# The first block's probabilities: transposed by a float32 matmul instead of by DMA, and new DMA durations in the ordering clock

## The chip, the cores and the metric

The kernel runs on one core of a Trainium2 chip. The metric is the device time of one execution in microseconds (us), lower is better. A core has five engines that work side by side, each in the order of its own queue: PE (matmuls; PEld is its weight load), DVE (vector work), ACT (activations and scaled copies), POOL (a second, slower vector engine) and SP, which here only issues DMA transfers.

## The reference

Causal attention, then a gated two-layer network on its output, all float32. Sizes: 4 batches, 12 heads, 448 positions, 64 per head; 1792 tokens of 768, hidden width 2048.

```python
scores = scale * np.matmul(q, k.transpose(0, 1, 3, 2))
scores = np.where(mask, -1000000000.0, scores)
scores = scores - np.max(scores, axis=-1, keepdims=True)
attn = np.exp(scores)
attn = attn / (np.sum(attn, axis=-1, keepdims=True) + 1e-09)
attn_out = np.matmul(attn, v)
x = attn_out.transpose(0, 2, 1, 3).reshape(B * S, H * D)
h = x @ w_in
g = h * (1.0 / (1.0 + np.exp(-1.702 * h)))
out = g @ w_out
```

## The kernel before

**Tiling.** The sequence of each batch is cut into two blocks, of 4 and of 3 chunks of 64 rows (`blocks`, eight in all, n = 0 to 7). A block has six units, one for each pair of heads (`unit`, L1134). The two heads of a pair lie in the two halves of the 128 partitions. After the attention of a block come its `h_slice`s (L1254: x times w_in, eight slices of 256 hidden columns, with the gate) and its `out_tile`s (L1307: g times w_out, tiles of 128 tokens in two halves of 384 columns). Products in the network and most in the attention are made of float16 pairs (a high part and a rest, "hi" and "lo", three matmuls for one).

**One unit.** For each run of two chunks: scores on PE into `ps_s` (L1060 in float32 for batch 0, L1068 in float16 pairs for the others), mask and row minimum on DVE into the float32 tile `z` (L1091), exponential and row sum on ACT (L1105), the sum scaled on POOL or DVE (L1163), its reciprocal on DVE (L1169). `p_pair` (L1117) then writes the probabilities, z times the reciprocal, as two float16 tiles in `p16`: hi on ACT or DVE (`scaled`, L476 or L478), lo on DVE (`rest`, L481). When all runs of the unit are there, one DMA transpose on SP's queue (L1179) turns `p16` into `PT`, and PE multiplies by the values (L1197, the "PV" matmuls) into `ps_v`. After every second unit ACT and DVE write `xT` (L1215 to L1224; for block 1 it is `xT1`). `p16` and `PT` have two buffers each, `z` has one place for each chunk, `ps_h` has three banks, which the `h_slice`s use.

**The weights.** They come in 64-bit words; `to_f32` (L555) makes float32 of them (L565 to L608, on ACT and DVE), `gram` (L621) estimates their size on PE, `split` writes float16 pairs. This runs beside the attention of the first two blocks, and loads on SP's queue feed it.

**What sets the order.** Nothing is ordered by hand. `Ops.add` takes each step with an estimated cost on the engines that could do it, its reads and writes, a priority from `TUNE` and, for transfers, a DMA duration. `Ops.order` (L107) searches 300 rounds over a list planner, with a DMA clock (`DMA_START`, `DMA_END`, `ROWS`, L73) and a PE clock, and emits each step on the engine that the best round gave it. So an altered cost can move steps everywhere, and from one engine to another.

Of the kernel before, what the change touches and what calls it, by code (L numbers as in the profile page):

```python
# [59 lines left out]
class Ops:  # L60
# [9 lines left out]
    HOP = 0.14  # L70
    SECOND = 1e5
    LOAD = 0.68
    DMA_START, DMA_END, DMA_DEPTH = 1.0, 0.8, 8  # L73
    ROWS = 0.19

    def __init__(self):
        self.ops = []
# [239 lines left out]
def pool(n, rate=1.885):  # L317
    return {"POOL": (rate * n + 220) / 1e3}
# [3 lines left out]
def kernel(  # L322
# [451 lines left out]
    def v_batch(b, prio):  # L774
        st = bst[b]
        for j in range(NJ):
            r = min(P, S - j * P)
            add(
                {"SP": Ops.LOAD},
                lambda e, j=j, r=r: nc.sync.dma_start(  # L780
                    out=vraw[:r, j], in_=v[b, :, j * P : j * P + r, :].rearrange("h p d -> p h d")
                ),
                [], [("vraw", j, 0)] + ([("vraw", j, 1)] if r == P else []), prio, dma=2.18 * r / P,
            )
        sqv, sqv_key = col("sqv", 2, 2 * NJ)
# [14 lines left out]
        if not (b == 0 and TUNE["gram_v"]):  # L800
            add(
                dve(2 * NJ),
                lambda e: nc.vector.tensor_reduce(out=sq, in_=sqv, axis=AX.X, op=ALU.max),
                [(sqv_key, j) for j in range(2 * NJ)], [sq_key], prio,
            )
        amx, amx_key = all_max(sq, sq_key, "v", "S" if b else "O", prio)
        st["s_v"], st["s_v_key"] = col("s_v", 2)
        st["i_v"], st["i_v_key"] = col("i_v", 2)
        norm_scale("v", amx, amx_key, st["s_v"], st["s_v_key"], st["i_v"], st["i_v_key"], prio)
# [67 lines left out]
    def k_unit32(u, c0, c1, prio):  # L877

        m = u % 2
        f = q16[:, m * 16 * D : m * 16 * D + 8 * D].bitcast(F32).rearrange("p (j t d) -> p j t d", j=2, d=D)  # L880
        w = 64 * (c1 - c0)
        r = w // 2
        keys = [("q16", m, j) for j in range(4)]
        load_heads(f, k[0, 2 * u : 2 * u + 2, 64 * c0 : 64 * c1], r, [keys[:2], keys[2:]], prio, 0.045 * (c1 - c0))
        got, got_key = turn(f, r, keys, prio)
        kt = kT[u // 2][:, u % 2 * NC : u % 2 * NC + NC].rearrange("p c w -> p (c w)").bitcast(F32)
        add(
            {**act(w, psum=True, rate=1.2), **dve(w, rate=1.2)},
            lambda e: scaled(e, kt[:, 64 * c0 : 64 * c1].rearrange("p (x t) -> p x t", t=2), got, 1.0),
            [got_key], [("kT", u, c) for c in range(c0, c1)], prio,  # L890
        )
        bst[0]["kT", u] = kt

    def q_unit32(n, u, prio):
# [3 lines left out]
        r = 32 * ni  # L898
        f = qf[:, i].rearrange("p (j t) d -> p j t d", j=2)
        keys = [("qf", i, j) for j in range(2)]  # L900
        load_heads(f, q[b, 2 * u : 2 * u + 2, 64 * c0 : 64 * c1], r, [[x] for x in keys], prio, 0.045 * ni)
        got, got_key = turn(f, r, keys, prio)
        t = qT_r.next()
        qt = qT[t].rearrange("p c w -> p (c w)").bitcast(F32).rearrange("p (c j w) -> p c j w", j=2, w=64)
# [63 lines left out]
    def q_pair(n, u, prio):  # L968
# [7 lines left out]
        for a in range(2):  # L976
            for j in range(2):
                keys += [("qf", a, j)]
                add(
                    {"SP": Ops.LOAD},  # L980
                    lambda e, a=a, j=j: nc.sync.dma_start(  # L981
                        out=f[64 * j : 64 * j + 64, a * ni : (a + 1) * ni],
                        in_=q[b, 2 * (u + a) + j, 64 * c0 : 64 * c1].rearrange("(c p) d -> p c d", p=64),
                    ),
                    [], keys[-1:], prio, dma=0.09 * ni,
                )
        sq, sq_key = col("sqq", 2)
        square_sum(
# [128 lines left out]
    def p_pair(i, pi, at, r, r_key, prio):  # L1117
# [13 lines left out]
            zs + [r_key] + keys[0], keys[1], prio,  # L1131
        )

    def unit(n, u, prio):  # L1134
        b, c0, c1 = blocks[n]
        ni = c1 - c0
# [13 lines left out]
        for i0 in range(c0 - c0 % 2, c1, 2):  # L1150
# [5 lines left out]
            for a, i in enumerate(run):  # L1156
# [11 lines left out]
            add(  # L1168
                dve(6 * ln), lambda e, ls=ls, rs=rs: nc.vector.reciprocal(rs, ls), l_keys, [r_key], prio  # L1169
            )  # L1170
            for a, i in enumerate(run):
                at = [where[i, J] for J in range(i // 2 + 1)]
                assert at == list(range(at[0], at[-1] + 1, at[1] - at[0] if at[1:] else 1))
                p_pair(i, pp_i, at, rs[:, a : a + 1], r_key, prio)
        ne = len(places)
        all_keys = [("PT", pi)]
        add(
            Ops.turned(2 * ne),
            lambda e: nc.sync.dma_start_transpose(  # L1179
                out=PT[pi][:, :ne].rearrange("p a g t -> p (a g) t"),  # L1180
# [281 lines left out]
```

## Time and profile before

| what | value |
|---|---|
| median of 3 runs | 640.23 us |
| the runs | 640.47, 640.23, 637.7 us |
| profiled execution, first to last instruction (its span) | 633.9 us |
| busy: PE / DVE / ACT / POOL | 582.6 / 422.4 / 357.2 / 96.6 us |
| mean granted clock of PE | 0.976 of full speed |

The profiled execution has no time of its own beside its span; the runs lie 3.8 to 6.6 us above that span, for what is outside the first and last instruction. Busy shares are means over a program whose stages differ: the strips of the page (busy tenths in 40 slices of about 16 us) show DVE high in the first third and PE high from then on. A granted clock below 1.00 is a mix of PE's two levels, 1.2 and 2.4 GHz.

### The profile page before, as it was taken

Reading aid. Unit: us, or ns where it says so; the run is one execution under the profiler, and the core shown is the slowest. Engines: PE = TensorE matmul, PEld = TensorE weight load, DVE = VectorE, ACT = ScalarE, POOL = GpSimd, SP = SyncE. Lnnn points to the kernel's source line nnn. Section 1 sums busy time; section 2 is a strip of 40 time slices with the busy share of each in tenths; the row PEclk is TensorE's granted clock in tenths of the full one; section 3 lists DMA queues with packets and bytes.
Section 4 is the critical chain, followed back from the end, with each engine's and each line's share of the span. In section 5 each row is a group of like instructions: output and inputs, shape, how many; then the busy total and the mean of one; then the engine's idle time right before and its main releaser. Section 6 shows DMA issues by size and latency. Waiting matters only on the chain. (4 is left out here: it accounts for less than half of the span.)

```text
span 633.9 us, 14759 instructions
## 1 busy us (share of the span) xinstructions
PE 582.6 (92%) x5723; PEld 439.5 (69%) x5723; DVE 422.4 (67%) x1128; ACT 357.2 (56%) x835; POOL 96.6 (15%) x235
## 2 busy tenths in 40 slices
PE   4777688978999999998999999999999999999997
PEld 3555466754588767876678667885679688777964
DVE  4999899999978898977498976769644213101300
ACT  4878888778657776758465565557343223012210
POOL 2233220043202124121021521001000000000000
PEclk9976689999999999999999999999999999999999
DMA  8999969678599687999847798627620040000000
GB/s 276 271 277 293 220 224 284 194 188 166 110 176 190 120 164 124 180 159 173 176 103 135 136 181 160 127 62 130 122 67 2 13 96 1 3 26 26 1 26 26
DMA packets 226407, 85.71 MB, mean 135 GB/s; under 512 B 207137, under 2 KB 216097, under 8 KB 226337
## 3 DMA queue, kind: packets, MB, share of 16 engines
q1 hardware_dynamic: 226336, 84.76, 62.7%
q8 instruction: 45, 0.74, 0.5%
q14 instruction: 26, 0.20, 0.1%
HBM read 41.68 MB, written 5.51 MB: 74 GB/s over the span
## 5 line engine op out<-in xcount | busy, mean ns | idle before, releaser
L1268 PE MATMUL ps_h<-xT,wib 128*128 128x192 f16 (+1 forms) x2304 | 239.3, 261 | 3.5 <-DVE gT L481 3.4
L1333 PE MATMUL ps_o<-wob,gT 128*128 128x384 f16 (+1 forms) x1536 | 233.8, 326 | 5.3 <-DVE wob L481 2.3
L1268 PEld LDWEIGHTS <-wib 128*128 128x128 f16 x2304 | 207.0, 98 | 31.8 <-issue 12.1
L1333 PEld LDWEIGHTS <-gT 128*128 128x128 f16 (+1 forms) x1536 | 131.4, 101 | 87.0 <-issue 12.6
L1105 ACT ACTIVATE z<-z,cols 128x320 f32<-128x320 f32 (+5 forms) x168 | 83.8, 500 | 47.1 <-DVE cols L1091 40.1
L1294 DVE SCALAR_TENSOR_TENSOR ps_h<-t,ps_h 128x512 f32<-128x512 f32 (+1 forms) x64 | 39.9, 624 | 76.5 <-ACT t L1289 76.3
L481 DVE SCALAR_TENSOR_TENSOR p<-z,cols,p 128x384 f16<-128x384 f32 (+3 forms) x168 | 82.6, 523 | 3.0 <-ACT p L476 1.9
L1091 DVE CUSTOM_DVE_ANT_0 z<-ps_s,mask,cols 128x384 f32<-128x384 f32 (+6 forms) x126 | 55.8, 478 | 30.1 <-PE ps_s L1068 30.1
L1289 ACT ACTIVATE t<-ps_h,cols 128x512 f32<-128x512 f32 (+1 forms) x64 | 40.1, 627 | 60.0 <-PE ps_h L1268 59.5
L476 ACT ACTIVATE p<-z,cols 128x128 f16<-128x128 f32 (+3 forms) x108 | 55.3, 538 | 15.4 <-DVE cols L1169 6.7
L1163 POOL TENSOR_SCALAR cols<-cols 128x2 f32<-128x2 f32 (+1 forms) x70 | 20.1, 287 | 208.6 <-ACT z L1105 207.7
L481 DVE SCALAR_TENSOR_TENSOR gT<-ps_h,gT 128x512 f16<-128x512 f32 (+1 forms) x64 | 39.6, 620 | 15.8 <-ACT gT L476 15.7
L476 ACT ACTIVATE gT<-ps_h 128x512 f16<-128x512 f32 (+1 forms) x58 | 31.1, 539 | 28.3 <-DVE ps_h L1294 28.1
L476 ACT ACTIVATE ob<-ps_o,cols 128x384 f32<-128x384 f32 x23 | 13.2, 575 | 59.8 <-PE ps_o L1333 59.8
L1197 PEld LDWEIGHTS <-v 128*64 128x64 f16 x864 | 38.4, 113 | 9.6 <-issue 7.6
L1197 PE MATMUL ps_v<-PT,v 128*64 128x192 f16 (+3 forms) x864 | 41.1, 243 | 4.1 <-DMA PT<-p 4.1
L1068 PE MATMUL ps_s<-kT,qT 128*64 128x192 f16 (+4 forms) x504 | 38.8, 277 | 2.4 <-DVE cols L1091 1.3
L1060 PE MATMUL ps_s<-kT,qT 128*128 128x64 f32 (+6 forms) x84 | 29.3, 468 | 2.6 <-DVE cols L1091 1.9
L1024 POOL TENSOR_SCALAR q<-q 128x512 f16<-128x512 f16 (+1 forms) x30 | 25.2, 841 | 43.0 <-ACT q L476 30.1
L1105 ACT ACTIVATION_READ_ACCUMULATOR z<-z,cols 128x1 f32 x168 | 31.7, 188 | 0.0
L476 ACT ACTIVATE wob<-wob 128x768 f32<-128x768 f32 (+1 forms) x19 | 20.8, 1095 | 15.6 <-DMA wob<-in_moe_w_in_dram 10.6
L1068 PEld LDWEIGHTS <-qT 128*64 128x64 f16 x504 | 19.6, 110 | 13.9 <-issue 9.9
(89 smaller groups left out, 541.1 us busy)
## 6 DMA issues: line engine op xcount, KB each, us to landing
wob<-in_moe_w_in_dram SPq DMA_DIRECT2D x16, 768.0 KB, 6.0
wob<-in_moe_w_out_dram SPq DMA_DIRECT2D x9, 768.0 KB, 5.5
vraw<-in_moe_w_out_dram SPq DMA_DIRECT2D x7, 768.0 KB, 5.4
out_dram<-ob SPq DMA_DIRECT2D x28, 192.0 KB, 2.1
vraw<-in_v_dram SPq DMA_DIRECT2D x12, 384.0 KB, 5.7
kf<-in_k_dram SPq DMA_DIRECT2D x36, 112.0 KB, 2.9
qf<-in_q_dram SPq DMA_DIRECT2D x48, 64.0 KB, 3.2
qf<-in_q_dram SPq DMA_DIRECT2D x48, 48.0 KB, 2.7
```

What stands on the lines that cost most here:

```text
L476: nc.scalar.activation(out=dst, in_=src, func=AF.Copy, scale=sc)
L481: nc.vector.scalar_tensor_tensor(out=dst, in0=src, scalar=sc, in1=hi, op0=ALU.mult, op1=ALU.subtract)
L1024: nc.gpsimd.tensor_scalar(out=dst, in0=src, scalar1=1.0, scalar2=1.0, op0=ALU.mult, op1=ALU.mult)
L1060: nc.tensor.matmul(ps, qt[:, i - c0].rearrange("p j w -> p (j w)"), kt[:, : 64 * (i + 1)], start=True, stop=True)
L1068: nc.tensor.matmul(ps[64 * j : 64 * j + 64], qt[:, g, i - c0, 64 * j : 64 * j + 64], kt[:, : i + 1, 64 * j : 64 * j + 64], start=(g == 0), ...
L1091: lambda e: nc.vector.tensor_tensor_reduce(out=z[:, :w], in0=ps, in1=mask[:, S - w :], scale=c, scalar=3.0e38, op0=ALU.add, op1=ALU.min, a ...
L1105: lambda e: nc.scalar.activation(out=z[:, :w], in_=z[:, :w], func=AF.Exp, bias=m, scale=-1.0, accum_out=l),
L1197: nc.tensor.matmul(ps[64 * j : 64 * j + 64, 64 * (first - c0) : w], vt[:, gv, J, j, :], PT[pi][:, at, gp, 64 * j : 64 * j + 64], start=(t ...
L1268: nc.tensor.matmul(ph[:, t], wib[:, sl, u, gw, t * P : (t + 1) * P], xT[x][:, gx, u, :w], start=(u == 0 and gw + gx == 0), stop=(u == NU - ...
L1289: lambda e: nc.scalar.activation(out=th, in_=ph, func=AF.Tanh, scale=ts[:, sl : sl + 1]),
L1294: lambda e: nc.vector.scalar_tensor_tensor(out=ph, in0=th, scalar=1.0, in1=ph, op0=ALU.add, op1=ALU.mult),
L1333: nc.tensor.matmul(po[o : o + m, :OH], gT[:, f, gg, 64 * r : 64 * r + m], wo_pair(f, gw, nh), start=(f == 0 and gg + gw == 0), stop=(f == ...
```

## The change

For block 0 alone (`TUNE["pet"]`), `p_pair` and the DMA transpose are left out, and `p_turned` is called once for each run of two chunks. POOL or DVE writes `diag`, an identity scaled by the reciprocals, into the same `p16` memory. PE multiplies each 128x128 tile of `z`, as the stationary operand, by `diag` in float32: 2 tiles for the first run of a unit, 4 for the second, into a `ps_h` bank. ACT or DVE copies the hi part from there to `PT`, DVE writes the lo part. That makes 12 runs and 36 such matmuls. `PT` now has four dependency keys instead of one. The second edit replaces the DMA durations that the ordering clock uses: start and end, rows of a transpose, and the loads of q, k and v.

```diff
@@ TUNE @@
+    pet=(0,),
@@ class Ops @@
-    DMA_START, DMA_END, DMA_DEPTH = 1.0, 0.8, 8
-    ROWS = 0.19
+    DMA_START, DMA_END, DMA_DEPTH = 1.23, 0.95, 8
+    ROWS = 0.214
@@ v_batch; k_unit32, q_unit32; q_pair @@
-... dma=2.18 * r / P,
+... dma=2.43 * r / P,
-load_heads(f, ..., 0.045 * ni)
+load_heads(f, ..., 0.062 * ni)
-[], keys[-1:], prio, dma=0.09 * ni,
+[], keys[-1:], prio, dma=0.125 * ni,
@@ new @@
+    def p_turned(run, pi, pp_i, where, rs, r_key, prio):
+        ...
+        add(
+            {**pool(ln * P), **dve(ln * P)},
+            lambda e: by(e).tensor_tensor(
+                out=diag,
+                in0=ident.unsqueeze(1).to_broadcast([P, ln, P]),
+                in1=rs.unsqueeze(2).to_broadcast([P, ln, P]),
+                op=ALU.mult,
+            ),
+            [r_key] + ident_keys, diag_keys, prio,
+        )
+        hb = ps_h_r.next()
+        ps = ps_h[hb][:, : nt * P]
+        def mm(e):
+            for at, J, a, i in tiles:
+                nc.tensor.matmul(
+                    ps[:, (at - p0) * P : (at - p0 + 1) * P], z_of(i)[:, J], diag[:, a], start=True, stop=True
+                )
+        add({"PE": nt * (4 * P / 2.4 + 150) / 1e3}, mm, ...)
+        ...
+        add({**act(nt * P, psum=True), **dve(nt * P)}, lambda e: scaled(e, hi, ps3, 1.0), ...)
+        add(dve(nt * P), lambda e: rest(lo, ps3, 1.0, hi), ...)
@@ unit @@
+            if n in TUNE["pet"]:
+                p_turned(run, pi, pp_i, where, rs, r_key, prio)
+                continue
...
-        all_keys = [("PT", pi)]
-        add(
+        all_keys = [("PT", pi, x) for x in range(4)]
+        if n not in TUNE["pet"]:
+          add(
             Ops.turned(2 * ne),
```

The planner then orders everything anew. In the rows that follow, names carry their buffer numbers, a line number of the changed kernel is higher by 1 up to its L1133 and by 48 or 52 behind `p_turned`, and `ISA` at L1091 (L1092) is the mask and row minimum, whose second row reads out the minimum.

DVE, where the first unit's probabilities are made. Before:

```order
L1169 RECIPROCAL cols_88<-cols_88 128x2
L603 SCALAR_TENSOR_TENSOR wob_61<-wob_61 128x768
L481 SCALAR_TENSOR_TENSOR p160_82<-z_81,cols_88,p160_82 128x128 x2
L1091 ISA z_81,cols_88<-ps_s0_91,mask_87 128x64
L1091 ISA cols_88 128x1
L632 TENSOR_REDUCE cols_88<-ps_o1_98 128x1
L481 SCALAR_TENSOR_TENSOR p160_82<-z_81,cols_88,p160_82 128x2x128
L1091 ISA z_81,cols_88<-ps_s0_91,mask_87 128x128
L1091 ISA cols_88 128x1
L1091 ISA z_81,cols_88<-ps_s1_92,mask_87 128x192
L1091 ISA cols_88 128x1
L481 SCALAR_TENSOR_TENSOR p160_82<-z_81,cols_88,p160_82 128x2x128
```

Now, from the reciprocals of the first unit on:

```order
L1217 RECIPROCAL cols_88<-cols_88 128x2 x2
L482 SCALAR_TENSOR_TENSOR wib_62<-wob_61,cols_88,wib_62 128x6x256
L633 TENSOR_REDUCE cols_88<-ps_o1_98 128x1
L579 TENSOR_SCALAR wob_61<-wob_61 128x768
L444 TENSOR_SCALAR cols_88<-cols_88 128x1
L479 TENSOR_SCALAR kT1_68<-ps_o0_97 128x256
L593 TENSOR_SCALAR wob_61<-wob_61 128x768
L1092 ISA z_81,cols_88<-ps_s0_91,mask_87 128x64
L1092 ISA cols_88 128x1
L1092 ISA z_81,cols_88<-ps_s0_91,mask_87 128x128
L1092 ISA cols_88 128x1
L604 SCALAR_TENSOR_TENSOR wob_61<-wob_61 128x768
```

Between the reciprocals and the second unit's write to `z` there stood two rests of `p16`; now a weight split and other weight work stand there, and the `z` row needs PE's matmuls on the old `z` behind it.

POOL, after its constants. Before:

```order
L542 MEMSET vraw_64 64x768
L1163 TENSOR_SCALAR cols_88<-cols_88 128x2 x2
L457 TENSOR_SCALAR cols_88<-cols_88 128x1
L450 TENSOR_SCALAR cols_88<-cols_88 128x1
L1163 TENSOR_SCALAR cols_88<-cols_88 128x2
L457 TENSOR_SCALAR cols_88<-cols_88 128x1
L450 TENSOR_SCALAR cols_88<-cols_88 128x1
L1163 TENSOR_SCALAR cols_88<-cols_88 128x2 x2
```

Now:

```order
L543 MEMSET vraw_64 64x768
L912 MEMSET qT1_78 64x4x64
L451 TENSOR_SCALAR cols_88<-cols_88 128x1
L1211 TENSOR_SCALAR cols_88<-cols_88 128x2
L1146 TENSOR_TENSOR p160_82<-ident_99,cols_88 128x256 x2
L458 TENSOR_SCALAR cols_88<-cols_88 128x1
L451 TENSOR_SCALAR cols_88<-cols_88 128x1
L1211 TENSOR_SCALAR cols_88<-cols_88 128x2
L1146 TENSOR_TENSOR p161_83<-ident_99,cols_88 128x256
```

The `TENSOR_TENSOR` rows are the scaled identities. They stand between the small scalar steps; 11 of the 12 are on POOL, one is on DVE.

SP, the first transfers. Before:

```order
L652 DMA wob_61<-in_moe_w_in_dram 128x3x512 x2
L856 DMA q16_76<-in_k_dram 128x128 x2
L856 DMA qf_74<-in_q_dram 128x128 x2
L856 DMA q16_76<-in_k_dram 128x128
L856 DMA qf_74<-in_q_dram 128x128
L856 DMA q16_76<-in_k_dram 128x128
L652 DMA wob_61<-in_moe_w_in_dram 128x3x512
L856 DMA qf_74<-in_q_dram 128x128
```

Now:

```order
L857 DMA qf_74<-in_q_dram 128x128 x2
L653 DMA wob_61<-in_moe_w_in_dram 128x3x512 x2
L857 DMA q16_76<-in_k_dram 128x128
L857 DMA qf_74<-in_q_dram 128x128 x2
L857 DMA q16_76<-in_k_dram 128x128 x2
L653 DMA wob_61<-in_moe_w_in_dram 128x3x512
L857 DMA q16_76<-in_k_dram 128x128
L653 DMA wob_61<-in_moe_w_in_dram 128x3x512
```

Two loads of q now stand ahead of the first weight loads, and the second load of the first unit's k (`q16` is its landing place) comes later in the row. Further down, SP's queue has lost six transposes of 12 tiles.

## Rows read from the trace of the kernel before

**Rows 1.** The page: granted clock and DMA share in 40 slices.
```profile
PEclk9976689999999999999999999999999999999999
DMA  8999969678599687999847798627620040000000
```
**Rows 2.** Windows: stretch, length, busy us by engine (count), clock, DMA share, GB/s.
```profile
core 0: us, PE busy (x) PEld busy (x) DVE busy (x) ACT busy (x) POOL busy (x), PEclk, DMA share, GB/s
16.00:32.00 16.00, 12.71 (x104) 9.65 (x104) 15.55 (x52) 13.99 (x38) 4.47 (x9) 1.00 1.14 272
64.00:80.00 16.00, 10.29 (x84) 7.44 (x84) 13.82 (x24) 13.23 (x25) 5.25 (x6) 0.68 0.99 228
16.00:80.00 64.00, 45.87 (x373) 34.63 (x371) 60.45 (x155) 52.78 (x119) 20.23 (x32) 0.79 1.09 266
85.40:182.50 97.10, 86.67 (x786) 62.04 (x785) 91.86 (x210) 75.79 (x151) 20.76 (x44) 0.98 0.82 198
182.50:634.00 451.50, 439.99 (x4477) 335.19 (x4474) 259.23 (x747) 215.76 (x548) 50.55 (x136) 1.00 0.52 98
```
**Rows 3.** Waits of PE, 16 to 182.5 us: total, times, longest.
```profile
PE ps_o L430 <- DVE cols L632: 7.6, 6, 2.8
PE ps_o L621 <- DVE wob L603: 4.9, 5, 1.5
PE ps_v L1197 <- DMA PT<-p: 3.0, 1, 3.0
```
**Rows 4.** Lines by form, 0 to 182.5 us: shapes, count, busy, mean ns, idle before.
```profile
L481 DVE SCALAR_TENSOR_TENSOR p<-z,cols,p 128x128 f16<-128x128 f32 x16 | 5.1, 342 | 0.0
L481 DVE SCALAR_TENSOR_TENSOR p<-z,cols,p 128x256 f16<-128x256 f32 x14 | 6.3, 479 | 0.1
L478 DVE TENSOR_SCALAR p<-z,cols 128x128 f16<-128x128 f32 x4 | 1.0, 281 | 0.0
L478 DVE TENSOR_SCALAR p<-z,cols 128x256 f16<-128x256 f32 x2 | 0.7, 352 | 0.0
L478 DVE TENSOR_SCALAR v<-vraw,cols 128x1024 f16<-128x1024 f32 x4 | 2.9, 753 | 0.1
L478 DVE TENSOR_SCALAR ob<-ps_o,cols 128x384 f32<-128x384 f32 x2 | 1.2, 606 | 0.0
L578 DVE TENSOR_SCALAR wob<-wob 128x768 uint16<-128x768 uint16 x9 | 5.4, 605 | 0.9 <-DMA wob<-in_moe_w_out_dram 0.8
L578 DVE TENSOR_SCALAR wob<-wob 128x1536 uint16<-128x1536 uint16 x4 | 4.1, 1037 | 0.4 <-DMA wob<-in_moe_w_in_dram 0.4
L481 DVE SCALAR_TENSOR_TENSOR wob<-wob,cols 128x768 f16<-128x768 f32 x16 | 16.5, 1034 | 0.7 <-ACT wob L476 0.6
L481 DVE SCALAR_TENSOR_TENSOR wib<-wob,cols,wib 128x1536 f16<-128x1536 f32 x8 | 14.5, 1810 | 1.1 <-ACT wib L476 1.1
```
**Rows 5.** The same of the whole span: rests read from PSUM.
```profile
L481 DVE SCALAR_TENSOR_TENSOR gT<-ps_h,gT 128x512 f16<-128x512 f32 x32 | 22.0, 687 | 6.9 <-ACT gT L476 6.9
L481 DVE SCALAR_TENSOR_TENSOR gT<-ps_h,gT 128x384 f16<-128x384 f32 x32 | 17.6, 554 | 8.9 <-ACT gT L476 8.8
```
**Rows 6.** Timeline of SP and PE: start, us, what, count, idle before.
```profile
3.05 1.21 SPq L856 DMA_DIRECT2D qf<-in_q_dram  x2
...
28.49 2.87 SPq L1179 DMA_TRANSPOSE PT<-p  x1
...
15.01 2.72 PE L1060 MATMUL ps_s<-kT,qT 128*128 128x64 f32 x8
...
25.05 0.71 PE L1060 MATMUL ps_s<-kT,qT 128*128 128x64 f32 x4 [0.24 <-ACT qT L476]
```
**Rows 7.** Timeline of POOL, and of DVE at the end of the second row.
```profile
57.28 1.53 POOL L1163 TENSOR_SCALAR cols<-cols 128x2 f32<-128x2 f32 x1 [2.10 <-ACT z L1105]
...
136.05 4.51 POOL L1024 TENSOR_SCALAR q<-q 128x512 f16<-128x512 f16 x1 [5.30 <-DVE q L481]
...
274.20 0.62 POOL L1024 TENSOR_SCALAR q<-q 128x512 f16<-128x512 f16 x1
...
140.00 1.37 DVE L481 SCALAR_TENSOR_TENSOR wob<-wob,cols 128x768 f16<-128x768 f32 x1
```
**Rows 8.** The chain that ended last: start, us, what; its last long piece.
```profile
604.01 26.34 PE ps_o L1333 x162
```

More of the change, by code (lines that the diff above doesn't have):

```diff
@@ L782, in v_batch @@
                 ),
-                [], [("vraw", j, 0)] + ([("vraw", j, 1)] if r == P else []), prio, dma=2.18 * r / P,
+                [], [("vraw", j, 0)] + ([("vraw", j, 1)] if r == P else []), prio, dma=2.43 * r / P,
             )
@@ L883, in k_unit32 @@
         keys = [("q16", m, j) for j in range(4)]
[L884 removed]
+        load_heads(f, k[0, 2 * u : 2 * u + 2, 64 * c0 : 64 * c1], r, [keys[:2], keys[2:]], prio, 0.062 * (c1 - c0))
         got, got_key = turn(f, r, keys, prio)
@@ L900, in q_unit32 @@
         keys = [("qf", i, j) for j in range(2)]
-        load_heads(f, q[b, 2 * u : 2 * u + 2, 64 * c0 : 64 * c1], r, [[x] for x in keys], prio, 0.045 * ni)
+        load_heads(f, q[b, 2 * u : 2 * u + 2, 64 * c0 : 64 * c1], r, [[x] for x in keys], prio, 0.062 * ni)
         got, got_key = turn(f, r, keys, prio)
@@ L1132, in p_pair @@
         )
+    def p_turned(run, pi, pp_i, where, rs, r_key, prio):
+        ln = len(run)
+        tiles = sorted((where[i, J], J, a, i) for a, i in enumerate(run) for J in range(i // 2 + 1))
+        p0, nt = tiles[0][0], len(tiles)
+        assert [t[0] for t in tiles] == list(range(p0, p0 + nt)) and 2 <= nt <= 4
+        diag = p16[pp_i][:, p0 : p0 + 2].rearrange("p a g w -> p (a g w)").bitcast(F32)
+        diag = diag.rearrange("p (a w) -> p a w", w=P)[:, :ln]
+        diag_keys = [("p16", pp_i, x, g) for x in (p0, p0 + 1) for g in range(2)]
+        add(
[16 more added lines that the diff above has]
+        add(
+            {"PE": nt * (4 * P / 2.4 + 150) / 1e3},
+            mm,
+            diag_keys + [k for i in run for k in z_keys(i)], [("H", hb)], prio,
+        )
+        ps3 = ps.rearrange("p (a w) -> p a w", w=P)
+        hi, lo = (PT[pi][:, p0 : p0 + nt, g] for g in range(2))
+        part = 2 * (p0 > 0)
+        add(
+            {**act(nt * P, psum=True), **dve(nt * P)},
+            lambda e: scaled(e, hi, ps3, 1.0),
+            [("H", hb)], [("PT", pi, part)], prio,
+        )
+        add(
+            dve(nt * P),
+            lambda e: rest(lo, ps3, 1.0, hi),
+            [("H", hb), ("PT", pi, part)], [("PT", pi, part + 1)], prio,
+        )
     def unit(n, u, prio):
@@ L1175, in unit @@
         ne = len(places)
-        all_keys = [("PT", pi)]
-        add(
+        all_keys = [("PT", pi, x) for x in range(4)]
+        if n not in TUNE["pet"]:
+          add(
             Ops.turned(2 * ne),
```

## The prediction

> **What bounds the kernel now.** I read the strips of the page first, then windows, then the waits, then the groups by form, and the timeline where a single duration was needed. The strips [rows 1] show the granted clock below full speed only early, and the DMA engines near full there too. The windows [rows 2] split the program at 182.5 us, where DVE writes the last piece of `xT1`, that is, where block 1's attention ends. Behind that point PE is busy 439.99 of 451.5 us: its work sets the end, and only 11.5 us of idle time are left to gain. Ahead of it DVE is the fullest engine: 15.55 of 16 us in the window from 16 to 32, 60.45 of 64 from 16 to 80, 91.86 of 97.10 from 85.4 to 182.5. PE has 64 - 45.87 = 18.1 us idle from 16 to 80, and it waits for DVE in the chains that scale the weights, and once 3.0 us for a transpose of probabilities [rows 3]. So the first 182.5 us are worth what they cost DVE, as long as PE keeps its backlog, and what PE has not done by then is paid for afterwards, us for us.
>
> The profiled execution has a span of 633.9 us; the median of the runs is 640.2, and I take the 6.3 us between them as unchanged. The sum below is a change of the span, put on 640.2.
>
> **The change part by part.**
>
> *DVE's own work in block 0.* Removed are 12 rests of one tile at 0.342 us and 12 of two tiles at 0.479 [rows 4], 9.85 us, and the two high parts that stood on DVE in this block, 0.281 + 0.352 = 0.63. The other 22 high parts were ACT's. Added are 12 rests read from PSUM, 6 of 512 and 6 of 256 columns. The nearest rows are the gate's rests from PSUM, 0.687 for 512 and 0.554 for 384 columns [rows 5]; 0.133 per 128 columns makes 0.421 for 256, an estimate. That is 6.65 us. Two high parts stand on DVE now, one of each size, taken at the same prices, 1.11, and one scaled identity at the 0.479 of a 256-column operation with two inputs. Together 8.24 against 10.48: **-2.2 us**. Ten of the 12 high parts are ACT's, which has 11 us idle from 16 to 80 [rows 2]; I cost them at nothing.
>
> *Steps that the new order gives to ACT.* I counted both orders on DVE up to the third row that writes `xT1`. Beside block 0's own, DVE has lost two high parts of `v` (0.753 each), two copies of `ob` (0.606), two weight steps at L578 of 768 columns (0.605) and one of 1536 (1.037), 4.97 us [rows 4]. It has gained the high part of a `wib` slice, which no DVE row shows: between 1.04 (the 1536-column row, one input) and 1.81 (the rest of a slice, two inputs); I take 1.04, for it has one input. That is **-3.9 us** (-3.2 at the other bound). Smaller steps of both signs are left out. ACT hides what it takes: it has 97.1 - 75.8 = 21 us idle from 85.4 to 182.5 [rows 2]. If it did not, the 3.9 would come back.
>
> *The transposes and SP's queue.* Six issues of about 2.9 us on SP [rows 6] and their transfers go. DVE waits for hardly any transfer, so I credit only the window from 64 to 80, where PE waited 3.0 us for a transpose [rows 3] and DVE was idle 16 - 13.82 = 2.18 us [rows 2]: **-2.2 us**, with zero as the other end. What is late next there is the weight work on DVE, which stands in the same queue.
>
> *The start.* Two loads of q now go out ahead of the first weights. Two such issues took 1.21 us [rows 6], and nothing on DVE can begin before weights land: **+1.2 us**, with zero as the other end.
>
> *The scaled identities on POOL.* No row has this operation. From below, a POOL copy of 512 columns of float16 took 0.62 us undisturbed; from above, the same kind took 4.51 us beside a run of DVE weight steps, and a scalar step of two columns took 1.53 [rows 7]. The disturbance goes both ways: the DVE row that stood at the end of those 4.51 us took 1.37 us, where its kind has a mean of 1.034 [rows 4, 7]. I let half of the 11 identities on POOL cost DVE 0.34 us each: **+1.9 us**, with zero and 11 x 0.62 = 6.8 as ends. The new wait: PE's matmuls on `z` wait for POOL, and behind them in PE's queue stand scores of later units; DVE waits for both, since its next write to `z` needs the matmuls done. The order puts a 1.81 us weight split and an L578 step of 0.605 between [rows 4], so 2.4 us of cover at the first unit, against two identities at 0.62 and one pair of matmuls at 0.71: covered.
>
> *PE's own work.* 36 float32 matmuls of 128 columns. Two float32 score matmuls of 64 and 128 columns took 0.71 us at full clock, 0.36 each; the four of 64 to 256 columns that ran at 15.01 took 2.72, 0.68 each [rows 6]. At 0.39 (0.36 and a little for the columns, an estimate) they are 14.0 us, which fit into the 18.1 us that PE is idle from 16 to 80 [rows 2]. So they are off the path, at nothing; if that cover is gone, see the third rival.
>
> *What is left for PE afterwards.* Ahead of the last PV matmuls of block 1, the order before has 29 groups of six `out_tile` matmuls, the new one 24; `h_slice` groups are 35 in both. A group is 6 x 26.34 / 162 = 0.976 us [rows 8], so **+4.9 us** of PE work lie behind the point, in the stage that PE bounds. With the 11.5 us of idle time there as the only cover, I count it in full; zero is the other end.
>
> **Sum:** -2.2 - 3.9 - 2.2 + 1.2 + 1.9 + 4.9 = -0.3, and with unrounded terms -0.4. Forecast: **639.8 us**, no difference that a measurement of this kernel can tell (0.5%, 3.2 us).
>
> **The rivals.**
>
> *Faster: the early gain arrives whole.* The five groups slip into PE's waits behind 182.5 us, where 11.5 us stand idle and DVE has less work to wait for, and the identities don't disturb DVE. Then 4.9 and 1.9 fall away: 639.8 - 6.8 = **633.0 us**. For it: DVE and DMA, the two fullest resources early, both lose work. Against it: the idle time there is scattered in waits of about a microsecond.
>
> *Slower: the identities are held up on POOL, and hold DVE up.* Cover at the first unit is 2.4 us; less 0.71 for the matmuls, two identities may take 0.85 us each. Beyond that point PE waits, and DVE behind it. If each of the 11 takes the 1.53 us that a scalar step took in this stage [rows 7], that is 11 x (1.53 - 0.85) = 7.5 us: **647.3 us**. For it: POOL was held for 4.51 us beside DVE's weight steps, and such steps fill this stage. Against it: later units have more DVE work between the reciprocal and its use. The Trainium skill ("SBUF — State Buffer", section "SBUF: two separate sides") states that DVE and GpSimd share one port pair as an exclusive lock, and that whichever operation starts first holds it for its whole length. By that rule, each identity that starts ahead of a two-input DVE operation would block it for all of its length; the 1.37 us row shows a third of a microsecond, not a whole operation, and the 4.51 us row agrees with it in the other direction.
>
> *Slower: PE becomes the bound of block 0.* If its clock stays as from 64 to 80, 0.68 granted, a mix of the levels 1.2 and 2.4 GHz [rows 2], the matmuls cost 0.68 each, 24.5 us, and only 18.1 are idle: +6.4, **646.2 us**. Against it: from 16 to 32 PE was busy 12.71 of 16 us and the clock was 1.00 [rows 2], and the change makes PE busier.
>
> That the change doesn't do what it says isn't likely, for the new order shows no transpose in block 0. That its new DMA durations make a worse order elsewhere would look like the five groups above, and lies in the range.
>
> **How the numbers follow.** Forecast 0.36, faster rival 0.33, POOL 0.18, PE 0.13. The low end of all bounds together is -6.2 - 2.2 = -8.4, 631.8 us; the high end is -2.2 - 3.2 + 1.2 + 6.8 + 4.9 = +7.5, 647.7, and the two slower rivals end at 646 and 647. Orders that differ all along the program are seldom equal in their waits, so I add a microsecond at either end: 631 to 649. The likeliest case alone holds 637 to 643. The cases of slower together have 0.31.
>
> **What would show it.** Right: DVE reaches the third write of `xT1` some 3 to 5 us earlier than 182.5 us; PE busy grows by about 14 us before 80; the window behind that point grows by about 5 us of PE work. POOL's identities near 0.6 to 1 us would clear POOL, and 1.5 us with PE waiting for POOL would mean the first slower rival. A granted clock still near 0.7 from 48 to 80 with PE full would mean the second. The prediction is wrong if the stage behind block 1's attention changes by more than its work, for then the order's waits there, which I took as they were, decided.

## The result, and the profile after

| | before | after |
|---|---|---|
| median | 639.23 us (637.7 to 640.47, 4 runs) | 621.47 us (620.39 to 621.78, 4 runs) |
| ratio | | 0.9736, 95% interval 0.9701 to 0.977 |
| span of the profiled execution | 633.9 us | 618.7 us |

The change makes the kernel 2.6% faster, 17.8 us. The prediction, 639.8 us with 631 to 649, is wrong: the time lies 9.5 us below its range.

The two profiled executions differ by 15.2 us. The other 2.6 us are spread, not work: every later run lists its own span, and the time is 1.7 to 2.2 us more, mostly 1.7 (627.75 with 625.9, 634.88 with 633.2). So the execution with the span of 633.9 us took about 635.6 (an estimate from these pairs), at the quick end of what the kernel before does (634.2 to 642.0 us in the runs of this study), and the 6.3 us that the prediction put outside the span were mostly that spread.

The strips of the page of the changed kernel, which answer to [rows 1]: the clock dips in one early slice only, and the DMA engines are less full there.

```profile
PEclk9999799999999999999999999999999999999999
DMA  8989569977699487979955897947633410000000
```

The windows, which answer to [rows 2]; the mark that splits them, the sixth row of DVE that writes `xT`, is now at 171.8 us, and the line up to it stands here for both kernels (first two lines of before, then after):

```profile
0.00:16.00 16.00, 6.53 (x48) 5.20 (x49) 6.92 (x12) 7.73 (x11) 4.34 (x20) 1.00 0.83 277
0.00:182.50 182.50, 142.66 (x1248) 104.27 (x1249) 163.18 (x383) 141.47 (x288) 46.08 (x99) 0.92 0.90 226
```
```profile
core 0: us, PE busy (x) PEld busy (x) DVE busy (x) ACT busy (x) POOL busy (x), PEclk, DMA share, GB/s
0.00:16.00 16.00, 5.08 (x41) 3.98 (x42) 6.11 (x10) 8.46 (x12) 4.33 (x20) 1.00 0.91 267
64.00:80.00 16.00, 13.65 (x122) 10.62 (x123) 15.89 (x27) 13.49 (x22) 3.19 (x10) 0.79 0.61 174
16.00:80.00 64.00, 48.77 (x481) 38.98 (x480) 61.74 (x147) 52.56 (x111) 28.91 (x44) 0.95 0.83 240
0.00:171.80 171.80, 136.09 (x1297) 103.58 (x1298) 157.19 (x355) 140.11 (x277) 55.77 (x110) 0.98 0.84 222
171.80:618.70 446.90, 442.30 (x4500) 338.12 (x4498) 261.57 (x758) 216.56 (x554) 49.90 (x135) 1.00 0.54 101
```

The 15.2 us fall into four pieces. Ahead of the mark, 10.7 us: DVE is busy 163.18 - 157.19 = 6.0 us less, and idle 19.3 - 14.6 = 4.7 us less. Of these 10.7 us, 5.6 are there when block 0's attention ends (the third row of DVE that writes `xT`, 85.4 and 79.8 us); the other 5.1 come in block 1, where no edited step stands, so they are the new order's. Behind the mark, 4.5 us: PE is busy 442.30 - 439.99 = 2.3 us more, and idle 4.6 instead of 11.4 us, 6.8 less. Nearly all of the last is in the waits of PE behind the mark, before first (total, times, longest):

```profile
PE ps_h L1268 <- DVE gT L481: 2.3, 3, 1.4
PE ps_o L1333 <- DVE ob L478: 1.6, 1, 1.6
PE ps_s L1068 <- DVE cols L1091: 1.3, 2, 1.0
PE ps_s L1068 <- DMA qT<-q: 1.2, 2, 1.0
PE ps_v L1197 <- DMA PT<-p: 1.2, 2, 0.8
...
```

After, one is left:

```profile
PE ps_s L1069 <- DVE cols L1092: 1.0, 1, 1.0
```

### The profile page after: what moved, and what is told of

The parts are those of the page before. It is cut to its first block, busy times and chain, and to the rows that moved or that the text cites. A ratio compares the mean times of both kernels' runs of the same rounds, so it can differ in the third digit from the quotient of the medians.

```text
span 618.7 us, 14859 instructions
## 1 busy us (share of the span) xinstructions
PE 578.4 (93%) x5795; PEld 441.7 (71%) x5795; DVE 418.8 (68%) x1112; ACT 356.7 (58%) x829; POOL 105.7 (17%) x245
## 5 line engine op out<-in xcount | busy, mean ns | idle before, releaser
L1385 PE MATMUL ps_o<-wob,gT 128*128 128x384 f16 (+1 forms) x1536 | 236.3, 326 | 2.8 <-ACT qT L477 1.6
L1106 ACT ACTIVATE z<-z,cols 128x320 f32<-128x320 f32 (+6 forms) x168 | 83.7, 499 | 55.4 <-DVE cols L1092 54.2
L482 DVE SCALAR_TENSOR_TENSOR p<-z,cols,p 128x384 f16<-128x384 f32 (+3 forms) x144 | 74.0, 539 | 3.7 <-ACT p L477 3.2
L1092 DVE CUSTOM_DVE_ANT_0 z<-ps_s,mask,cols 128x192 f32<-128x192 f32 (+6 forms) x126 | 55.8, 477 | 18.6 <-PE ps_s L1069 18.5
L1211 POOL TENSOR_SCALAR cols<-cols 128x2 f32<-128x2 f32 (+1 forms) x71 | 24.5, 345 | 210.7 <-ACT z L1106 209.6
L477 ACT ACTIVATE p<-z,cols 128x256 f16<-128x256 f32 (+3 forms) x90 | 47.7, 548 | 12.4 <-DVE cols L1217 7.8
L482 DVE SCALAR_TENSOR_TENSOR gT<-ps_h,gT 128x512 f16<-128x512 f32 (+1 forms) x64 | 39.7, 620 | 14.6 <-ACT gT L477 14.4
L477 ACT ACTIVATE gT<-ps_h 128x512 f16<-128x512 f32 (+1 forms) x53 | 28.8, 544 | 24.3 <-DVE ps_h L1346 24.1
L1069 PE MATMUL ps_s<-kT,qT 128*64 128x64 f16 (+4 forms) x504 | 38.8, 277 | 1.1 <-DVE cols L1092 1.0
L1025 POOL TENSOR_SCALAR q<-q 128x512 f16<-128x512 f16 (+1 forms) x31 | 21.6, 700 | 44.7 <-ACT q L477 26.9
L1061 PE MATMUL ps_s<-kT,qT 128*128 128x192 f32 (+6 forms) x84 | 25.4, 416 | 3.5 <-DVE cols L1092 2.6
```

The source lines that it names most:

```text
L477: nc.scalar.activation(out=dst, in_=src, func=AF.Copy, scale=sc)
L482: nc.vector.scalar_tensor_tensor(out=dst, in0=src, scalar=sc, in1=hi, op0=ALU.mult, op1=ALU.subtract)
L1061: nc.tensor.matmul(ps, qt[:, i - c0].rearrange("p j w -> p (j w)"), kt[:, : 64 * (i + 1)], start=True, stop=True)
L1069: nc.tensor.matmul(ps[64 * j : 64 * j + 64], qt[:, g, i - c0, 64 * j : 64 * j + 64], kt[:, : i + 1, 64 * j : 64 * j + 64], start=(g == 0), ...
L1092: lambda e: nc.vector.tensor_tensor_reduce(out=z[:, :w], in0=ps, in1=mask[:, S - w :], scale=c, scalar=3.0e38, op0=ALU.add, op1=ALU.min, a ...
L1106: lambda e: nc.scalar.activation(out=z[:, :w], in_=z[:, :w], func=AF.Exp, bias=m, scale=-1.0, accum_out=l),
```

## The experiments

The question was where 15 us come from when the prediction had found 0.4. Theory A is that the matmul transposes give them (DVE's work, the DMAs, PE's clock), B that the new DMA durations do, by an order with fewer waits, and C that the order search drew a good order by luck. Later pairs of theories stand in the expectations. The "mark" is that sixth `xT` row; the idle time of PE behind it is the length of the window from the mark to the end, less PE's busy time in it. Each ratio is to the kernel before, run beside it on the same chip, with its 95% interval. There the kernel before took 636.5 to 638.2 us in the median, so the times in the tables compare by their ratios and not with the 639.23. A mark comes from one profiled execution; in the kernels further down that have the same steps up to the mark it came at 182.0 and 182.8 instead of 182.5, and at 172.3 instead of 171.8.

### The two edits apart, and two seeds of the order search

The search starts from `SEED = 2`. Eight kernels separate its luck from the edits: the matmul transposes with the old DMA durations, the new durations with all transposes left as DMAs, both and neither, each from seed 2 and from seed 3. As an edit of the changed kernel, the first is

```diff
-    DMA_START, DMA_END, DMA_DEPTH = 1.23, 0.95, 8
-    ROWS = 0.214
+    DMA_START, DMA_END, DMA_DEPTH = 1.0, 0.8, 8
+    ROWS = 0.19
```

with the loads' durations set back likewise. Of the kernel before, the second is the reverse, and the seeds are `SEED = 3`.

> The matmul transposes of block 0 with the old DMA durations in the ordering clock; the order is searched anew, the program computes the same. Theory A (the transposes' work gives the gain: less DVE work and no DMA transposes ahead of the end of block 1's attention, with TensorE at the full clock there): 620 to 626 us, the third row of xT1 at 172 +- 2 us of the span. Theory B (the DMA durations give it, by an order that leaves PE fewer waits behind block 1's attention): 633 to 640 us before any gain on DVE, with PE idle some 10 us behind the milestone, not 4.6. Theory C (which order the search happens to end on): anything from 618 to 642, in no relation to the two parts.

> The kernel before with the new DMA durations in the ordering clock alone; all transposes stay DMAs. Theory A: 636 to 642 us, the third row of xT1 at 180 to 185 us. Theory B: 625 to 633 us, with PE idle behind the milestone down from 11.5 to about 5 us and the milestone still at 180 to 183. Theory C: anything from 618 to 642.

> The changed kernel with another seed of the order search (3 for 2), nothing else. Theories A and B: 619 to 626 us, for the work and the costs are the same and a search from another start should come within 1%. Theory C: more than 6 us from 621.5, on the slow side since the change's own seed may be a good draw: 628 to 640.

> The kernel before with another seed of the order search (3 for 2), nothing else. Theories A and B: 635 to 643 us. Theory C: more than 6 us from 639.2, so 625 to 633 us if the kernel before was a poor draw, or 646 and more.

> The matmul transposes of block 0 with the old DMA durations, order search from seed 3. Reading so far: the DMA durations decide PE's idle time behind the mark (9.5 to 11.4 us with the old ones in three orders, 3.8 to 5.0 us with the new ones in three), the transposes decide the mark, and the seed moves the mark by several us. Theory E (each part keeps its effect in another order): PE idle behind the mark 9 to 12 us, the mark at 172 to 179 us, 626 to 631 us where before stands at 637. Theory C (the luck of the search is as large as either part): PE idle behind the mark under 7 us, or the mark at 182 us and later.

> The new DMA durations alone, DMA transposes everywhere, order search from seed 3. Theory E: PE idle behind the mark 3.5 to 6 us, the mark at 181 to 185 us, 627 to 632 us. Theory C: PE idle behind the mark 8 us and more, or the mark under 178 us.

| transposes of block 0, durations, seed | time | ratio | span | mark | PE idle behind |
|---|---|---|---|---|---|
| DMA, old, 2 (before) | 639.23 us | 1 | 633.9 us | 182.5 us | 11.4 us |
| DMA, old, 3 | 635.9 | 0.9987 (0.9965 to 1.0009) | 634.4 | 181.6 | 11.0 |
| matmul, old, 2 | 628.16 | 0.9876 (0.9849 to 0.9902) | 625.9 | 175.6 | 9.6 |
| matmul, old, 3 | 632.21 | 0.9916 (0.9884 to 0.9947) | 630.3 | 171.1 | 13.1 |
| DMA, new, 2 | 629.39 | 0.9896 (0.9869 to 0.9923) | 627.1 | 183.9 | 3.7 |
| DMA, new, 3 | 626.74 | 0.9836 (0.9798 to 0.9873) | 624.7 | 177.7 | 6.0 |
| matmul, new, 2 (after) | 621.47 | 0.9736 (0.9701 to 0.977) | 618.7 | 171.8 | 4.6 |
| matmul, new, 3 | 628.55 | 0.9881 (0.9856 to 0.9907) | 627.0 | 180.2 | 5.1 |

Neither edit alone gives the gain, and each shows in its own column. With the old durations PE stands idle 9.6 to 13.1 us behind the mark, with the new ones 3.7 to 6.0, whatever the transposes and the seed: means of 11.3 and 4.9, so 6.4 us. The matmul transposes bring the mark from a mean of 181.4 to one of 174.7 us, 6.7 us, but here the search scatters: 171.1 to 180.2 in one group, 177.7 to 183.9 in the other. What does not overlap is DVE's busy time up to the mark: 157.2 to 161.0 us in the four kernels with matmul transposes, 162.0 to 163.4 in the other four; the means differ by about 4 us. Behind the mark PE is busy 2.1 us more in the mean with them, so over the whole span they are worth 4.6 us in the mean of their four pairs, from +8.4 to -2.3, and the durations 6.8, from 3.3 to 9.7.

So theories A and B each have a part, and C has one too: with another seed the span of the changed kernel is 8.3 us longer (627.0 us), all of it ahead of the mark, as C expected. The one order of seed 2 is a good draw: in the mean of both seeds the two edits together give 11.3 of the 15.2 us. Several expectations missed besides: the matmul transposes alone, seed 2, lie between A's range and B's; with seed 3 they came just past the ends of E's ranges; and the mark of 177.7 us with new durations and seed 3 fell where C had it.

### Ahead of the mark, in a fixed order

Here the order of before or of after is kept as it is, and one thing in it is altered.

Matmuls that nobody waits for, beside the scores of block 0 in the order before:

```diff
+            fill()
+        def fill():
+            for _ in range(3 if n == 0 else 0):
+                nc.tensor.matmul(ps_h[2][:, :P], ident, ident, start=True, stop=True)
```

> The kernel before in its own order, with three float32 128x128 matmuls of the identity by itself into an unused bank of ps_h behind each of the 12 score groups of block 0: 36 matmuls, as many as the change adds, with nobody waiting for them. Theory K (the granted clock: before has 30.7 us at the half clock ahead of its mark, the sixth xT row at 182.5 us, and the change 6.8 us; what PE does late at the half clock is what DVE waits for): the half clock falls under 15 us and the mark comes 3 to 5 us earlier, 631.5 to 634 us. Theory D (the gain ahead of the mark is DVE's own work and the DMA transposes; PE's clock is a by-product): the extra 10 to 14 us of PE lie ahead of scores in PE's queue, the mark stays or comes up to 3 us later, 636 to 640 us.

The 36 transposing matmuls of after, made short:

```diff
-                    ... z_of(i)[:, J], diag[:, a], start=True, stop=True
+                    ... z_of(i)[:, J].bitcast(BF16)[:, 1::2], diag[:, a].bitcast(BF16)[:, 1::2], ...
```

> The changed kernel in its own order, its 36 transposing matmuls on the bfloat16 upper halves of probabilities and diagonal (one short pass each, probabilities of lower precision), all waits as they were. PE loses some 10 us of work ahead of 80 us. Theory K: the half clock comes back (6.8 us to 15 us and more) and the mark, 171.8 us, comes 2 to 5 us later: 622 to 626 us on this chip, where the changed kernel should stand near 620. Theory D: the way from the exponentials to PT gets shorter and the mark comes 0 to 2 us earlier: 618 to 620 us.

The six DMA transposes of block 0, left out of the order before (`PT` filled with ones once by two DVE instructions at the start):

```diff
-            lambda e: nc.sync.dma_start_transpose(
+            lambda e: n and nc.sync.dma_start_transpose(
```

> The kernel before in its own order without the six DMA transposes of block 0 (its probabilities are left out: PT is filled with ones once at the start). DVE's work and PE's stay. My forecast had 2.2 us for this part (DVE idle between 64 and 80 us). Theory D: the mark comes 2 to 5 us earlier, with the PT waits of PE (3.0 us) gone: 631 to 634.5 us. Theory K: DVE and PE keep their pace, 0 to 1 us: 635.5 to 637 us.

The low parts of `PT` twice on DVE, in the order of after:

```diff
-            lambda e: rest(lo, ps3, 1.0, hi),
+            lambda e: [rest(lo, ps3, 1.0, hi) for _ in range(2)],
```

> The changed kernel in its own order with each of the 12 low parts of PT computed twice on DVE (0.40 or 0.70 us each, 6.6 us in all, the same result). Theory D (DVE bounds the stage ahead of the mark, as the forecast's sum has it): the mark comes 5 to 6.6 us later, 625 to 627 us where the changed kernel stands near 620. Theory K (DVE follows PE there): 0 to 3 us later, 620 to 623 us.

| | time | ratio | mark | DVE busy to the mark | DVE idle to the mark |
|---|---|---|---|---|---|
| before | 639.23 us | 1 | 182.5 us | 163.2 us | 19.3 us |
| with 36 idle matmuls | 634.52 | 0.9945 (0.9922 to 0.9969) | 180.6 | 162.8 | 17.8 |
| without the six DMA transposes | 633.02 | 0.9915 (0.9874 to 0.9956) | 178.7 | 165.0 | 13.7 |
| after | 621.47 | 0.9736 (0.9701 to 0.977) | 171.8 | 157.2 | 14.6 |
| with short matmuls | 620.5 | 0.9713 (0.9677 to 0.9749) | 171.0 | 157.1 | 13.9 |
| low parts twice | 626.03 | 0.9796 (0.9761 to 0.9831) | 177.5 | 163.0 | 14.5 |

The last row settles what bounds this stage: 5.8 us more on DVE, and the mark comes 5.7 us later with the same idle time. Theory K expected the mark 2 to 5 us later with the short matmuls, which it is not. The windows of that kernel and of after from 48 to 64 us show PE at the lower of its two levels, 1.2 GHz, all through in the first and at 2.4 in the second, and DVE just as full:

```profile
48.00:64.00 16.00, 13.71 (x92) 9.90 (x92) 15.82 (x36) 14.26 (x29) 10.44 (x14) 0.50 0.76 256
```
```profile
48.00:64.00 16.00, 11.29 (x122) 8.54 (x122) 15.81 (x36) 15.04 (x31) 10.58 (x14) 1.00 0.79 262
```

Its mark comes 0.8 us earlier, not 2 to 5 later. PE had less work there too, so what this shows is that PE at the lower level kept up with DVE in this order; no run changes the clock alone. The six DMA transposes are worth 3.8 us at the mark: DVE's idle time falls by 5.6 us, of which the two filling instructions use 1.9 in the first 16 us. The window in which the prediction looked for it, 64 to 80 us, fills up as it said (13.82 us busy in [rows 2]):

```profile
64.00:80.00 16.00, 11.28 (x117) 8.37 (x116) 15.93 (x27) 15.88 (x31) 5.97 (x9) 0.79 0.60 137
```

That DVE gains 3.7 us behind 16 us, and not only these 2.1, is the prediction's shortfall. All of it is there at the end of block 0's attention (81.6 instead of 85.4 us). The idle matmuls fit neither theory: 1.9 us at the mark, with a clock that is hardly better (0.76, 0.82 and 0.68 in the three windows from 32 to 80 us, against 0.77, 0.69 and 0.68). Block 0's attention ends as before (85.3 and 85.4 us), so the 1.9 us come behind the stage in which these matmuls stand. What makes them stays open.

### Behind the mark: which of the new durations, and how

> The kernel before with only the start and end of a DMA set anew in the ordering clock (1.23 and 0.95 for 1.0 and 0.8), the sizes of the loads and of the transposes' rows left. These 0.38 us apply to every DMA, the 36 transposes of PT behind the mark among them, which the order of before starts too late (8 of 36 PV groups begin within 4.0 us of the transpose's issue). If the ends give the gain: PE idle behind the mark 4 to 6 us, 628 to 632 us. If the sizes give it: 9 to 12 us idle, 634 to 640 us. Half each: 7 us, 632 to 635 us.

> The kernel before with only the sizes set anew (q and k loads, v loads, 0.214 for 0.19 us a row of a transpose), start and end of a DMA left. If the ends give the gain: PE idle behind the mark 9 to 12 us, 634 to 640 us. If the sizes give it: 4 to 6 us idle, 628 to 632 us.

Only start and end anew: 627.24 us, 0.9843 (0.981 to 0.9877), mark 176.7, PE idle behind it 9.9 us. Only the sizes anew: 629.55 us, 0.9873 (0.9835 to 0.9911), mark 180.1, idle 6.4 us. So the sizes take most of the idle time away: 6.4 us lies just above the range of the new durations in the table of eight, 9.9 inside that of the old ones. The other kernel is as fast by an earlier mark, which one order cannot tell from the scatter seen above; with that much idle time 634 to 640 us were expected, so its time alone would have misled.

Then the transfers themselves. In the orders of before and after, DMA transposes behind the mark are left out:

```diff
-            lambda e: nc.sync.dma_start_transpose(
-                out=PT[pi]...
+            lambda e: n > 1 or nc.sync.dma_start_transpose(
+                out=PT[pi]...
```

and in two of three kernels also the q loads and the transposes of `qT`, in the same way with `n > 2`.

> The kernel before in its own order, without the DMA transposes of PT in blocks 2 to 7 and without the q loads and qT transposes of blocks 3 to 7 (the tiles keep what an earlier block left there, so those blocks compute with old q and probabilities). Theory L (late DMAs: PE behind the mark waits, directly or through ACT and DVE, for DMAs that the old order starts too late): PE idle behind the mark falls from 11.4 to 4 to 6 us, and 631 to 633 us where before stands at 637.5. Theory M (a better arrangement of the engines, DMAs have no part): 9.5 to 11.5 us idle, 635.5 to 638 us.

> The changed kernel in its own order with the same DMAs left out (PT in blocks 2 to 7, q and qT in blocks 3 to 7). Both theories: there is little left to gain, PE idle behind the mark 4.6 us falls by 0 to 1 us: 619 to 621 us where the changed kernel stands near 620.5. A fall by more than 2 us would say that leaving DMAs out gains by itself, whatever the order, and would weaken what e13 can show.

> The kernel before in its own order, without the DMA transposes of PT in blocks 2 to 7 alone (old probabilities are used there). Theory L, with the PT transposes as the late ones (8 of 36 PV groups begin within 4.0 us of the issue): PE idle behind the mark 5 to 7 us, 632 to 634 us. Theory L with q loads and qT as the late ones: 8.5 to 10.5 us, 634.5 to 637 us. Theory M: 9.5 to 11.5 us, 635.5 to 638 us.

| | time | ratio | mark | PE idle behind |
|---|---|---|---|---|
| before, without PT, q and qT | 627.57 us | 0.9849 (0.9822 to 0.9876) | 182.0 us | 3.9 us |
| before, without PT | 627.91 | 0.9847 (0.9819 to 0.9874) | 182.8 | 4.3 |
| after, without PT, q and qT | 620.27 | 0.9733 (0.971 to 0.9757) | 172.3 | 3.7 |

Theory L holds, and the transposes of `PT` are what it needs. Without them the old order has as little idle time as the new one; the new one, with 4.6 us, loses only 0.9 by the same cut. Both kernels came out faster than L had it (631 to 633 and 632 to 634 us): the idle time fell by 7.1 to 7.5 us and the time by 10, for the profiled execution of before was one of its quickest. What its slower ones lose more is in no trace. All of PE's waits behind the mark in the old order without `PT`, against the five lines above:

```profile
PE ps_o L1333 <- DVE ob L478: 0.3, 1, 0.3
PE ps_h L1268 <- DVE gT L481: 0.2, 1, 0.2
PE ps_s L1068 <- DVE cols L1091: 0.2, 1, 0.2
```

So the waits that the profile of before put down to DVE's `gT`, `ob` and row minima came from the transposes too, one or two steps removed. These runs don't separate two ways: a transpose that lands late, and loads that stand behind it in SP's queue. For ACT's waits for q loads behind the mark fall as well, from 8.5 to 1.6 us, though only `PT` is left out. The timeline of before shows one case of the first way (start, us, what, idle before):

```profile
184.02 1.43 SPq L1179 DMA_TRANSPOSE PT<-p  x1
...
187.99 0.28 DVE L478 TENSOR_SCALAR p<-z,cols 128x128 f16<-128x128 f32 x1 [1.00 <-DMA PT<-p]
188.00 0.40 ACT L476 ACTIVATE p<-z,cols 128x128 f16<-128x128 f32 x1 [1.41 <-DMA PT<-p]
...
189.18 0.63 ACT L466 ACTIVATE waste<-qf 128x512 bf16<-128x512 f32 x1 [0.78 <-DMA qf<-in_q_dram]
...
189.93 0.15 DVE L443 TENSOR_SCALAR cols<-cols 128x1 int32<-128x1 int32 x1 [0.94 <-ACT waste L466]
...
191.62 0.56 DVE L1294 SCALAR_TENSOR_TENSOR ps_h<-t,ps_h 128x384 f32<-128x384 f32 x1
...
192.73 0.56 DVE L481 SCALAR_TENSOR_TENSOR gT<-ps_h,gT 128x384 f16<-128x384 f32 x1 [0.56 <-ACT gT L476]
...
193.34 0.90 PE L1268 MATMUL ps_h<-xT,wib 128*128 128x192 f16 x9 [1.40 <-DVE gT L481]
```

The transpose issued at 184.02 us reads `p16` until 187.99. ACT and DVE wait to write that buffer again, 1.41 and 1.00 us; the steps in their queues behind it slip, the gate's among them, and PE waits 1.40 us for the `ps_h` bank. There is a q load in this chain as well, and it stays when `PT` is left out; PE's gap at this place is then 0.22 us.

What the figures of the clock are against the trace: the 36 transposes of `PT` behind the mark in before, and below them its 62 q loads there, land so long after the start of their issue (least, median, most):

```profile
DMA to landing us min/median/max: 3.7/4.9/6.6
```
```profile
DMA to landing us min/median/max: 2.1/2.5/5.6
```

With no other transfer ahead of it, the old clock reckons 1.0 + 2 x 0.19 x 6 + 0.8 = 4.1 us for a transpose of 12 tiles and 5.6 for one of 20, the new one 4.7 and 6.5. The 4.9 us mixes both sizes. Taken apart, the 18 of 12 tiles took 3.7, 4.1 and 5.5 us (least, median, most), the 18 of 20 tiles 4.8, 5.1 and 6.6. So for the transposes the old figures are not short of the middle, and the new ones are a margin for the late ones. For a q load of four chunks the old clock has 1.0 + 0.09 x 4 + 0.8 = 2.2 us, near the least, and the new one 2.7, above the median. The order made with the new figures leaves PV more room. With the old ones the first PV matmul of a unit starts within 0.1 us of the landing in 3 of the 36 units behind the mark, and less than 3.9 us after the end of the issue in 8; in the changed kernel the least is 1.5 us behind the landing and 4.1 us behind the issue.

Which new figure does it stays open. The sizes of the loads and of the transposes' rows were changed together. As far as one order each can tell, the transposes' figures alone don't explain it: the new start and end put 0.38 us on each, more than the sizes put on one of 12 tiles (0.29), and left 9.9 us idle.

### A try at a faster version

The low parts moved off DVE, by an ACT copy and a POOL subtraction:

```diff
-            dve(nt * P),
-            lambda e: rest(lo, ps3, 1.0, hi),
+            act(nt * P, psum=True),
+            lambda e: scaled("ACT", copy, ps3, 1.0),
...
+            pool(nt * P),
+            lambda e: nc.gpsimd.tensor_tensor(out=lo, in0=copy, in1=hi, op=ALU.subtract),
```

> A try at a faster version: the changed kernel with the low parts of block 0's PT taken off DVE. ACT copies each PSUM group once more, in float32 to a free part of p16, and POOL subtracts the high part (12 of each); the order is searched anew. DVE loses 6.6 us ahead of the mark. If DVE's work alone decides: the mark at 166 to 168 us and 614 to 617 us. If the longer way (PE, ACT, ACT, POOL) or POOL's rate holds PV back, or the new order is a poorer draw: the mark at 170 to 176 us, 619 to 626 us.

627.62 us, 0.9834 (0.9798 to 0.987), mark 176.6 us, just past the worse of the two ranges. The 6.6 us went back to DVE in two ways. The new order gave it other steps, and the same steps took longer beside POOL's. DVE's weight steps up to the mark, after first (shapes, count, busy, mean ns):

```profile
L482 DVE SCALAR_TENSOR_TENSOR wib<-wob,cols,wib 128x1536 f16<-128x1536 f32 x8 | 14.5, 1815 | 0.1
L604 DVE SCALAR_TENSOR_TENSOR wob<-wob 128x1536 int32<-128x1536 int32 x5 | 8.8, 1753 | 0.0
```
```profile
L482 DVE SCALAR_TENSOR_TENSOR wib<-wob,cols,wib 128x1536 f16<-128x1536 f32 x8 | 15.5, 1934 | 1.8 <-ACT wib L477 1.8
L604 DVE SCALAR_TENSOR_TENSOR wob<-wob 128x1536 int32<-128x1536 int32 x5 | 10.4, 2080 | 0.0
```

Over all lines and shapes that both this kernel and before have, the longer means add up to 3.9 us; for the changed kernel the same sum is 0.6 us. DVE is busy 157.7 us to the mark, no less than after, and idle 18.9 instead of 14.6. Nothing here beats the changed kernel: the short matmuls (0.9713) lie within its interval, at a lower precision.

## Why the prediction was wrong, by its own steps

**What bounds the kernel: right.** DVE ahead of the mark, us for us, as the doubled low parts show; PE behind it, though there its waits counted as well as its work.

**DVE's own work and the steps given to ACT, -2.2 and -3.9: right in the sum.** DVE is busy 6.0 us less to the mark, 3.6 of it in block 0's stage and 2.4 in block 1's. The estimated price of a 256-column rest from PSUM, 0.421 us, was 0.410 (rows of after by form):

```profile
L482 DVE SCALAR_TENSOR_TENSOR PT<-ps_h,PT 128x512 f16<-128x512 f32 x6 | 4.1, 682 | 0.0
L482 DVE SCALAR_TENSOR_TENSOR PT<-ps_h,PT 128x256 f16<-128x256 f32 x6 | 2.5, 410 | 0.0
```

**The transposes and SP's queue, -2.2: too small.** Leaving the six out of the old order gives 3.8 us at the mark. The prediction credited one window where DVE's idle time stood beside a wait of PE for `PT`; the rest was in other idle times of DVE that no row ascribes to a transpose.

**The start, +1.2: near.** DVE's idle time in the first 16 us grows from 9.08 to 9.89 us, 0.8.

**The identities on POOL, +1.9: about half of it came.** They take (least, median, most, ns)

```profile
L1146 POOL TENSOR_TENSOR p<-ident,cols x11: 612/614/2165, 21.3 to 68.0; 128x256 f32<-128x256 f32 x11
```

and DVE's same steps 0.6 us more in all. Step by step, four of DVE's steps that start during an identity run 0.1 to 0.4 us over the least of their kind, 1.0 us together; this is inside the busy time above. PE waits for the identities, as the next line shows; of DVE's waits from 16 us to the mark none is for the transposing matmuls.

```profile
PE ps_h L1159 <- POOL p L1146: 5.0, 5, 2.1
```

So the first slower rival falls. The second, PE as the bound, falls by the doubled low parts, which move the mark us for us, and by PE's sum: the 36 matmuls took 12.2 us where 14.0 were reckoned, and from 16 to 80 us PE is busy only 2.9 us more, for its other work there took 36.6 us at a clock of 0.95 instead of 45.9 at 0.79.

**The groups left for PE, +4.9: too large.** By the traces 179 `out_tile` matmuls start ahead of the mark before and 156 after, 3.8 groups and not five, and PE's busy time behind the mark grows by 2.3 us.

**PE's waits behind the mark, taken as they were: the step that failed.** The prediction wrote that 11.5 us of idle time were left there and that an order made with new DMA durations might be worse; it gave their effect no term. It was -6.8 us, the largest of all, and it came with the new durations in all four pairs (6.4 us in the mean). The profile of before held a sign of it: behind the mark the landing of a `PT` transpose ended waits of PE (1.2 us), ACT (2.2) and DVE (1.3). The prediction's last sentence on what would show it wrong names this case, the waits of the order; it should have been a rival with a price.

**The sum, again.** In the two traces: -6.0 (DVE's work), +0.8 (start), -5.5 (DVE's other idle time: 3.7 of it by the old order without transposes, the rest this order's), +2.3 (PE behind the mark), -6.8 (its waits) = -15.2 us. The prediction's terms up to the mark, -2.2 - 3.9 - 2.2 + 1.2 + 1.9 = -5.2, stand near the mean of the four pairs, -6.7; the order that was drawn gave -10.7. That part is luck: the changed kernel from seed 3 stands at 0.9881, which of 639.23 us would be 631.6, inside the range, and the waits behind the mark would have been wrong all the same (5.1 us). The faster rival (633.0) had the direction, but with other reasons: it let the groups slip into the idle time, which went away instead.

## What to carry to other kernels

Where a search orders the program by its own clock, a changed duration in that clock is an edit of its own: compare each figure with the trace (here, issue to landing, each size by itself) before calling it free, and look for its effect wherever the bounding engine waits, also for waits that are booked to another engine. A wait's releaser is the last link only; leaving the suspected transfers out of the same order shows what they hold up in all, if not by which way. And one order is one draw: two seeds of each arm cost little and moved the mark of one kernel by up to 8.4 us, more than any term of the sum.

## What the runs showed of the hardware

Two-input steps of DVE lengthen beside POOL's tensor operations: in the last kernel the 1536-column step at L604 took 2080 instead of 1753 ns in the mean when POOL had 12 more of them, and these took 1284 and 1464 ns in the mean for 256 and 512 columns. Which side pays shows step by step (start, us, what):

```profile
79.78 1.79 DVE L482 SCALAR_TENSOR_TENSOR wib<-wob,cols,wib 128x1536 f16<-128x1536 f32 x1
81.50 2.71 DVE L604 SCALAR_TENSOR_TENSOR wob<-wob 128x1536 int32<-128x1536 int32 x1
79.97 2.62 POOL L1187 TENSOR_TENSOR PT<-p,PT 128x512 f16<-128x512 f32 x1 [2.23 <-ACT p L477]
```

DVE's first step began ahead of POOL's and took its usual 1.8 us, and POOL's took 2.62 us, 1.46 over the 1.16 of the shortest of its kind. DVE's second step began while POOL's still ran, for another 1.09 us, and took 0.96 us more than its usual 1.75. So the one that began second paid, nearly in full. This agrees with the Trainium skill ("SBUF — State Buffer", section "SBUF: two separate sides": the engine that starts first keeps the shared port pair for the whole instruction).

In the early stage, where DVE bounds, 16 us of TensorE at the lower of its two levels, with less work on PE, left DVE as full and the mark where it was (171.0 and 171.8 us). Whether the kernel before loses anything by its lower clock there, no run shows.
